# Chunk 1 of the first feed-forward layer in seven block products, with weight sums ahead, x inside `big`, and a new planned order

## Chip, core and metric

The kernel runs on one core of a Trainium2 chip: TensorE (PE, with its weight loads shown as PEld), VectorE (DVE), ScalarE (ACT), GpSimd (POOL) and SyncE (SP, which only issues DMAs here). The metric is the device time of one execution in microseconds (us). The kernel before took 268.82 us, the median of three runs between 268.78 and 269.34.

## What is computed

Four layers on x, 2048 tokens of 512 in bf16: linear attention, feed-forward, and both again with the same weights (wqkv 512 x 1536, wo 512 x 512, w1 512 x 1376, w2 1376 x 512).

```python
def _A_ref(x, wqkv, wo):          # 32 heads of 16
    qkv = (x @ wqkv).reshape(B, S, 3, H, Dh).transpose(2, 0, 3, 1, 4)
    q, k, v = qkv[0], qkv[1], qkv[2]
    phi = lambda t: jnp.where(t > 0, t + 1, jnp.exp(t)) + 1e-6
    pq, pk = phi(q), phi(k)
    kv = jnp.einsum("bhsd,bhse->bhde", pk, v)
    z = jnp.einsum("bhsd->bhd", pk)
    num = jnp.einsum("bhqd,bhde->bhqe", pq, kv)
    den = jnp.einsum("bhqd,bhd->bhq", pq, z)[..., None] + 1e-6
    return (num / den).transpose(0, 2, 1, 3).reshape(B, S, D) @ wo

def _B_ref(x, w1, w2):
    h = jnp.maximum(jnp.einsum("bsd,df->bsf", x, w1), 0)
    return jnp.einsum("bsf,fd->bsd", h, w2)

x = x + _A_ref(_layernorm(x), wqkv, wo)
x = x + _B_ref(_layernorm(x), w1, w2)
x = x + _A_ref(_layernorm(x), wqkv, wo)
x = x + _B_ref(_layernorm(x), w1, w2)
```

## The kernel before

**Tiles and tensors.** The tokens lie in 16 tiles of 128 tokens, four tiles to a chunk. `xin` holds x as loaded, `xres` the running sum in f32, `xn` the normalised tokens in f16, `Tb` the same transposed. `big` holds 48 units of 128 x 512 in bf16: pk and pq in attention (units 0 to 31), the spread reciprocals in units 32 to 47, and in a feed-forward layer h, where unit `c * 4 + t` is block c of 128 features for chunk t (c runs from 0 to 10, the last one with 96 features). `escr` and `lnd` are scratch.

**Attention** (layers 0 and 2): `a_k` and `a_q` project with wqkv and `phi_evac` evacuates from PSUM: ACT writes x + 1 (`_lin`) and exp (`_exp`), DVE takes the minimum (`_em`) and the maximum (`_phi`). `a_g` sums pk against the tokens over all chunks, `bar` closes these sums and forms `Mf` from them (`a_g_evac`, `a_kv`, `a_m` with its mask on DVE at L728, evacuation at L735 and L736). `a_den` forms the denominators, `a_spread` spreads their reciprocals by DMA (L783), `a_pqs` multiplies pq by them (L789), and `a_fin_chunk` multiplies by `Mf` and adds to the stream (`resid`, L660), with squares on ACT (L668) and the statistics and norms of the next layer (`ln_half`, `ln_stats` L572 to L584, `ln_norm` L590 to L599, transposes by DMA at L604).

**Feed-forward** (layers 1 and 3): a chunk's h = relu(x w1) is made either by `b_h`, block by block (four matmuls of 512 columns for each of ten blocks, relu at L964 or L965), or by `b_h7`, which cuts tokens, inputs and features in two each and needs seven block products instead of eight (a Strassen-Winograd scheme). For this it forms four sums of the tokens (`hs1` to `hs4`, L888) and four sums of w1 (`usum1` to `usum4`, L866), saves three products from PSUM by ACT (L926), adds in PSUM and by DVE (L913) and applies the relus (L916, L917, L943, L945). Each product has 10 matmuls of 256 columns. The 96 features left over go through `b_h_rest` and a DMA transpose (L844). The second half, h times w2, is always in seven products (`b_out`), with sums of h (`ssum1` to `ssum5`, `ssumr`) and of w2 (`wsum1` to `wsum6`; these two kinds at L983, the sign change `wsum6` at L995), and evacuations at L1066, L1074, L1082 and L1085. `H7_FROM = 2`: in layer 1 chunks 0 and 1 go through `b_h`, chunks 2 and 3 through `b_h7`; layer 3 uses `b_h7` throughout. The sums of w1 and w2 are written over `xin` once it is dead, apart from `usum3` and `wsum3`, which overwrite a quarter of w1 and of w2.

**Order.** The program records operations with what they read and write (`_Graph`), each with an assumed duration, and `_list_schedule` then puts them in an order for each engine: at each step, of the first so many operations not yet issued on an engine (`WINDOW`), by priority, the one that can start first. The priority is the place in the program plus an entry of the table `HINTS`; an entry with "!" fixes the engine of an operation that may run on several (`add_flex`: the number counts the alternatives). Operations with names in `LOCKED` are kept from running on DVE and POOL at the same time in that plan. Each engine then runs its list strictly in order, waiting on semaphores. `layer_steps` gives steps with what they need, so that the layers interleave.

Of the kernel before, what the change touches and what calls it, by code (L numbers as in the profile page):

```python
# [7 lines left out]
ALU = alu_op_type.AluOpType  # L8
# [38 lines left out]
TAIL = {PE: 150.0, ACT: 125.0, DVE: 80.0, POOL: 40.0, SP: 0.0}  # L47
# [4 lines left out]
WINDOW = {PE: 64, ACT: 80, DVE: 80, POOL: 12, SP: 6}  # L52


HINTS = {"0.bnag10": 2, "0.bnag14": 17, "0.bnst10": -271, "0.bnst12": 80, "0.bnst14": 51, "0.bnst15": 33, "0.bnst6": -82,
# [294 lines left out]
def build_kernel(nc, A_x, A_wqkv, A_wo, B_w1, B_w2, out, n_layers_pairs=2, K_STT=0, Q_STT=0, windows=None,  # L350
# [14 lines left out]
    EPS = 1e-5  # L365
    INV_D = 1.0 / D
    NLAYERS = 2 * n_layers_pairs
    UNITS = max(8 + 4, NFC) * NCH

    es = contextlib.ExitStack()  # L370
    with es:
# [14 lines left out]
        NL = 2  # L386
        FIN_SPLIT = 4
        SPLIT_H = 4
        H7_FROM = 2
        MID_FIRST = ()  # L390
        MID_LAST = ()
        FIRST_ACT_TILES = 4
# [1011 lines left out]
```

## Time and profile before

| | |
|---|---|
| median of the runs | 268.82 us (268.78 to 269.34) |
| the profiled execution | 269.65 us, of which the span of instructions is 267.9 us |
| matmuls and weight loads | 2020 each |
| DVE, ACT, POOL instructions | 612, 420, 158 |
| DMA | 22.18 MB, 83 GB/s mean |
| DMA issues on SP | three of wqkv and six of x in the first 6 us, 32 spreads, 28 transposes of `xn`, 8 of `hr` |

All times in the text count from the first instruction of the span. "busy" sums may overlap: a matmul's record is longer than the distance to the next one, because matmuls are pipelined. An idle engine costs nothing by itself; what counts is whether the engine that sets the end waits.

### The profile page before, as it was taken

To read this page: it belongs to the slowest core of one execution; us is meant where nothing else is said; L and a number is where in the kernel's file an instruction comes from. 1 tells how busy PE (TensorE), PEld (TensorE's weight loads), DVE (VectorE), ACT (ScalarE), POOL (GpSimd) and SP (SyncE) were. 2 spreads that over 40 slices of the span, in tenths; PEclk is the share of its full clock that TensorE was granted. 3 is DMA by queue.
4 is the path that set the end of the run, shared out by engine and by line. 5 is a ranking of instruction groups with operands and counts; after the bars stand their busy time and mean duration, and the time that the engine had idled before them with its cause. 6 is when DMAs were issued, how large, how long until landed. Compare 5 with 4: busy or idle time off the path is not lost.

```text
span 267.9 us, 5482 instructions
## 1 busy us (share of the span) xinstructions
PE 262.3 (98%) x2020; PEld 183.8 (69%) x2020; DVE 220.5 (82%) x612; ACT 192.0 (72%) x420; POOL 62.8 (23%) x158
## 2 busy tenths in 40 slices
PE   7999999999999999999999999999999999999995
PEld 3665446744646798768687745764488788898884
DVE  5799695679998799698889676348998989899994
ACT  4999987475994467689947599687899886475600
POOL 3210000015678014204005440000760830000000
PEclk9999999999999999999999999999999999999999
DMA  6904490644992400502202222063273221511012
GB/s 201 356 9 92 71 305 0 157 110 88 246 129 51 91 20 4 98 4 39 39 2 39 42 40 39 0 142 96 57 144 79 40 42 42 134 22 78 2 78 81
DMA packets 44890, 22.18 MB, mean 83 GB/s; under 512 B 34784, under 2 KB 43328, under 8 KB 44864
## 3 DMA queue, kind: packets, MB, share of 16 engines
q1 hardware_dynamic: 44864, 21.83, 34.5%
q8 instruction: 16, 0.26, 0.4%
q14 instruction: 10, 0.08, 0.1%
HBM read 7.14 MB, written 2.10 MB: 34 GB/s over the span
## 4 chain that ended last, share of the span: by engine, by line
PE 79%; ACT 8%; DMA 6%; DVE 5%; issue 0%; SPq 0%; DVEq 0%
PE ps L653 79%; DMA Tb<-xn 3%; ACT big L636 2%; ACT sqscr L668 2%; DMA wvl<-in_A_wqkv_dram 2%; DVE xres L660 2%; DMA xin<-in_A_x_dram 1%; ACT escr L638 1%; DVE big L789 1%; ACT Tb L624 1%; ACT xn L599 1%; DVE xn L590 1%; DVE bst L552 1%; ACT xres L638 1%; DVE xn L594 0%
## 5 line engine op out<-in xcount | busy, mean ns | idle before, releaser
L636 ACT ACTIVATE big<-ps 128x512 bf16<-128x512 f32 x64 | 39.7, 644 | 6.1 <-PE ps L653 5.8
L653 PE MATMUL ps<-Tb,w 128*128 128x256 f16 (+1 forms) x216 | 35.8, 304 | 0.1
L668 ACT ACTIVATE sqscr<-xres 128x512 bf16<-128x512 f32 x48 | 30.0, 626 | 6.9 <-DVE xres L1085 4.2
L653 PE MATMUL ps<-w,big 128*128 128x256 bf16 (+1 forms) x256 | 32.4, 272 | 0.0
L653 PE MATMUL ps<-wqkv,Tb 128*128 128x512 bf16 x128 | 31.2, 379 | 0.6 <-DMA Tb<-xn 0.6
L653 PE MATMUL ps<-big,xn 128*128 128x256 bf16 (+1 forms) x224 | 31.6, 288 | 0.0
L653 PE MATMUL ps<-Tb,wqkv 128*128 128x512 f16 (+1 forms) x144 | 31.4, 355 | 0.0
L638 ACT ACTIVATE escr<-ps 128x512 bf16<-128x512 f32 x48 | 29.9, 637 | 1.1 <-PE ps L653 1.1
L653 PE MATMUL ps<-Mf,big 128*128 128x512 bf16 x128 | 29.5, 379 | 0.0
L926 ACT ACTIVATE escr<-ps 128x512 f32<-128x512 f32 (+1 forms) x40 | 20.3, 540 | 11.2 <-PE ps L653 10.9
L653 PEld LDWEIGHTS ps<-w,big 128*128 128x128 bf16 (+1 forms) x256 | 25.0, 98 | 3.7
L653 PEld LDWEIGHTS ps<-big,xn 128*128 128x128 f16 x224 | 21.4, 98 | 8.8 <-issue 0.7
L653 PEld LDWEIGHTS ps<-Tb,w 128*128 128x128 bf16 x216 | 20.8, 98 | 9.5 <-DMA Tb<-xn 1.0
L913 DVE TENSOR_TENSOR big<-ps,escr 128x512 bf16<-128x512 f32 (+1 forms) x40 | 24.0, 606 | 3.7 <-PE ps L653 1.8
L599 ACT ACTIVATE xn<-xres,nbias,rstd 128x512 f16<-128x512 f32 x19 | 15.2, 810 | 9.6 <-POOL nbias L584 6.7
L653 PEld LDWEIGHTS ps<-Tb,wqkv 128*128 128x128 bf16 x144 | 13.9, 98 | 11.9 <-issue 0.2
L653 PEld LDWEIGHTS ps<-Mf,big 128*128 128x128 bf16 x128 | 12.2, 98 | 14.0 <-issue 0.7
L916 ACT ACTIVATE big<-big 128x512 bf16<-128x512 bf16 (+1 forms) x34 | 19.0, 569 | 3.2 <-DVE big L913 2.9
L646 DVE TENSOR_TENSOR big<-big,escr 128x512 bf16<-128x512 bf16 x48 | 19.8, 420 | 1.6 <-ACT big L636 1.1
L653 PEld LDWEIGHTS ps<-wqkv,Tb 128*128 128x128 f16 x128 | 12.1, 98 | 12.8 <-ACT escr L638 1.1
L1066 DVE TENSOR_TENSOR xres<-ps,xres 128x512 f32<-128x512 f32 x24 | 16.4, 685 | 4.6 <-PE ps L653 4.5
L640 DVE TENSOR_SCALAR escr<-escr 128x512 bf16<-128x512 bf16 x48 | 13.7, 287 | 7.7 <-ACT escr L638 7.2
(116 smaller groups left out, 525.2 us busy)
## 6 DMA issues: line engine op xcount, KB each, us to landing
big<-rdc SPq DMA_DIRECT2D x32, 128.0 KB, 2.6
wqkv<-in_A_wqkv_dram SPq DMA_DIRECT2D x3, 512.0 KB, 6.8
xin<-in_A_x_dram SPq DMA_DIRECT2D x3, 512.0 KB, 7.6
w<-in_B_w_dram SPq DMA_DIRECT2D x1, 1376.0 KB, 6.3
w<-in_B_w_dram SPq DMA_DIRECT2D x1, 1280.0 KB, 7.1
wo<-in_A_wo_dram SPq DMA_DIRECT2D x1, 512.0 KB, 7.2
out_dram<-GT SPq DMA_DIRECT2D x1, 512.0 KB, 2.6
out_dram<-Mf SPq DMA_DIRECT2D x1, 512.0 KB, 2.6
```

What stands on the lines that cost most here:

```text
L599: (ACT, lambda e: e.activation(xn[:, i, :], src, ACTF.Identity, scale=rstd[:, i:i + 1], bias=nbias[:, i:i + 1]), C_ACT_SB_AP)],
L636: g.add(ACT, lambda e: e.activation(dst_ap, psv[:, b, :], ACTF.Identity, bias=1.0 + 1e-6, scale=1.0), [("ps", b)], [dst_key], C_ACT_PSUM, ...
L638: g.add(ACT, lambda e: e.activation(sap, psv[:, b, :], ACTF.Exp), [("ps", b)], skeys, C_ACT_EXP, name=name + "_exp")
L640: g.add(DVE, lambda e: e.tensor_scalar(sap, sap, 1.0, 1e-6, ALU.min, ALU.add), skeys, skeys, C_DVE_BF4X, name=name + "_em")
L646: g.add(DVE, lambda e: e.tensor_tensor(dst_ap, dst_ap, sap, ALU.max), [dst_key] + skeys, [dst_key], 340.0, name=name + "_phi")
L653: last = e.matmul(o, l, r, start=st, stop=sp, skip_group_check=skip)
L660: g.add(DVE, lambda e: e.scalar_tensor_tensor(xres[:, i, :], psv[:, b, :], 0.0, src, ALU.add, ALU.add, accum_out=s1[:, i:i + 1]), [("ps", ...
L668: g.add(ACT, lambda e: e.activation(sqscr[:, q, :], xres[:, i, :], ACTF.Square, scale=math.sqrt(INV_D), accum_out=s2[:, i:i + 1]), xr(i), ...
L913: g.add(DVE, lambda e: e.tensor_tensor(ap, sh(psv[:, bank, 0:w]), sh(other()), ALU.add), [("ps", bank)] + okeys + ([] if first else bk), q ...
L916: g.add_flex([(ACT, lambda e: e.activation(ap, ap, ACTF.Relu), C_ACT_PSUM if len(cs) == 2 else 270.0), (DVE, lambda e: e.tensor_scalar(ap, ...
L926: g.add(ACT, lambda e, w=w: e.activation(q[:, 0:w], psv[:, bank, 0:w], ACTF.Identity), [("ps", bank)], key, C_ACT_PSUM if len(cs) == 2 els ...
L1066: g.add(DVE, lambda e: e.tensor_tensor(dst, psv[:, bank, :].rearrange("p (a k) -> p a k", k=256), dst, ALU.add), [("ps", bank)] + keys, ke ...
```

## The change

1. `H7_FROM` goes from 2 to 1: in layer 1 chunk 1 too goes through `b_h7`.
2. The sums of w1 have a tensor of their own, `tws`, those of w2 another, `tw2s`. All of them but `usum3` move from layer 1 into `bar` of layer 0; `usum3` stays ahead of chunk 1's `b_h7`.
3. `xin` is no tensor of its own any more but units 32 to 47 of `big`. h's blocks 8 to 10 lie there (`h_key` makes their writers wait for the readers of x), and the spread reciprocals move from there to the tiles of `Tb` of the same chunk (`rb_ap`).
4. `pqs`, `hs`, `ssum`, `usum` and `wsum` may run on DVE or POOL, a norm on DVE, ACT or POOL (before: every fourth on POOL, the others on DVE or ACT). `pool_tt` is the planner's assumed duration for POOL.
5. The planner's constants change (end of a matmul 150 to 160, a norm on DVE 530 to 470, POOL's window 12 to 40), and so does the place of layer 1's steps: its first is recorded after layer 0's third chunk instead of the second, and its first output step has no condition any more.
6. `HINTS` is replaced (494 entries before, 443 after).

```diff
-TAIL = {PE: 150.0, ACT: 125.0, DVE: 80.0, POOL: 40.0, SP: 0.0}
+TAIL = {PE: 160.0, ACT: 125.0, DVE: 80.0, POOL: 40.0, SP: 0.0}
-WINDOW = {PE: 64, ACT: 80, DVE: 80, POOL: 12, SP: 6}
+def pool_tt(cols):
+    return 2.2 * cols + 90.0
+WINDOW = {PE: 64, ACT: 80, DVE: 80, POOL: 40, SP: 6}
...
-    UNITS = max(8 + 4, NFC) * NCH
+    UNITS = 8 * NCH + NT
-        xin = sb("xin", [128, NT, 512], BF16)
-        H7_FROM = 2
+        H7_FROM = 1
+        xin = big[:, 8 * NCH * 512:UNITS * 512].rearrange("p (n d) -> p n d", d=512)
+        tws = sb("tws", [128, 3 * 1280], BF16)
+        tw2s = sb("tw2s", [128, 4096], BF16)
+        def h_key(u):
+            return [("big", u)] + ([("xin", u - 8 * NCH)] if u >= 8 * NCH else [])
...
-            if i % 4 == 3:
-                g.add(POOL, ts[1], xr(i) + [("rstd", i), ("mean", i)], [("xn", i)], ts[2], name="norm%d" % i)
-                return
-            g.add_flex([(DVE, ts[1], 530.0),
-                        (ACT, lambda e: e.activation(...), C_ACT_SB_AP)],
+            g.add_flex([(DVE, ts[1], 470.0),
+                        (ACT, lambda e: e.activation(...), C_ACT_SB_AP), ts],
...
-        def rb_unit(t, j):
-            return 32 + 4 * j + t
+        def rb_ap(t, j):
+            return Tb[:, 4 * t + j, :, :].rearrange("p c k -> p (c k)").bitcast(BF16)
-                    [("rdc", t)], [("big", u)], 650.0, "spread%d_%d" % (t, j), issue=620.0, late=late)
+                    [("rdc", t)], [("T", 4 * t + j)], 650.0, "spread%d_%d" % (t, j), issue=620.0, late=late)
+                f = (lambda e, u=u, j=j: e.tensor_tensor(unit_ap(u), unit_ap(u), rb_ap(t, j), ALU.mult))
+                g.add_flex([(DVE, f, 340.0), (POOL, f, pool_tt(512))], [("T", 4 * t + j), ("big", u)], [("big", u)], name="pqs%d_%d" % (t, j))
...
-        def w1_sums():
+        def w1_sums(part):
...
+                if (nm == "usum3") == (part == 0) and part < 2:
+                    continue
+                f = (lambda e, o=o, a=a, b=b: e.tensor_tensor(o, a, b, ALU.subtract))
+                g.add_flex([(DVE, f, C_DVE_SUM), (POOL, f, pool_tt(1280))], rd, wr, name=nm)
...
-                g.add(DVE, lambda e, o=o, a=a, b=b, op=op: e.tensor_tensor(o, a, b, op), rd, [wr], 340.0, name="%s_%d" % (nm, t))
+                f = (lambda e, o=o, a=a, b=b, op=op: e.tensor_tensor(o, a, b, op))
+                g.add_flex([(DVE, f, 340.0), (POOL, f, pool_tt(512))], rd, [wr], name="%s_%d" % (nm, t))
...
         def tt(out_, a, b, op, reads, writes, dur, name):
-            g.add(DVE, lambda e: e.tensor_tensor(out_, a, b, op), reads, writes, dur, name=name)
+            cols = {C_DVE_SUM: 1280, 450.0: 768, 340.0: 512, 200.0: 256}[dur]
+            f = (lambda e: e.tensor_tensor(out_, a, b, op))
+            g.add_flex([(DVE, f, dur), (POOL, f, pool_tt(cols))], reads, writes, name=name)
...
                 def bar():
                     g_a(NCH - 1)
+                    if first_layer:
+                        tw7.append(w1_sums(2 if H7_FROM == 0 else 0))
+                        w2_sums()
...
-                    if first_b and t == 0:
-                        w2_sums()
                     b_out(t, last_layer, sums[t])
...
                     if last_layer or t >= H7_FROM:
-                        if not tw7:
-                            tw7.append(w1_sums())
+                        if first_b and t == H7_FROM and t > 0:
+                            w1_sums(1)
                         b_h7(t, tw7[0])
...
-                    steps.append((1 if first_b and t == 0 else t, None, lambda t=t: h_step(t)))
+                    steps.append((2 if first_b and t == 0 else t, None, lambda t=t: h_step(t)))
                     if t >= 1:
-                        steps.append((NCH - 1 if first_b and t == 1 else None, None if last_layer else t - 1, lambda t=t: o_step(t - 1)))
+                        steps.append((None, None if last_layer else t - 1, lambda t=t: o_step(t - 1)))
```

The entries of the table that fix a sum on POOL are `hs1_3`, `hs3_2`, `hs4_1`, `ssum3_3`, `ssum4_0`, `ssumr_3` in layer 1 and `hs1_2`, `hs2_3`, `hs3_2`, `hs4_2`, `ssum4_0`, `ssum4_1`, `ssum5_2`, `ssumr_0` in layer 3 (the last number is the chunk). Of the loads, w1 loses its entry (231 before), w2's goes from 424 to 198, wo's from 239 to 156, wvl's from 164 to 190, and x's last quarter gets 146.

More of the change, by code (lines that the diff above doesn't have):

```diff
@@ L51 @@
 C_POOL_ADD = 1250.0
-WINDOW = {PE: 64, ACT: 80, DVE: 80, POOL: 12, SP: 6}
-HINTS = {"0.bnag10": 2, "0.bnag14": 17, "0.bnst10": -271, "0.bnst12": 80, "0.bnst14": 51, "0.bnst15": 33, "0.bnst6": -82,
[74 rows of a table removed]
+def pool_tt(cols):
+    return 2.2 * cols + 90.0
+WINDOW = {PE: 64, ACT: 80, DVE: 80, POOL: 40, SP: 6}
+HINTS = {"0.bnag11": 144, "0.bnst10": 103, "0.bnst8": 75, "0.bnst9": 111, "0.den1": 95, "0.fin0_2": -280, "0.fin14_0": 193,
[66 rows of a table added]
 class _Op:
@@ L367, in build_kernel @@
     NLAYERS = 2 * n_layers_pairs
-    UNITS = max(8 + 4, NFC) * NCH
+    UNITS = 8 * NCH + NT
+    assert NFC * NCH <= UNITS
     es = contextlib.ExitStack()
@@ L594, in ln_norm @@
             ts = (POOL, lambda e: e.tensor_scalar(xn[:, i, :], src, mean[:, i:i + 1], rstd[:, i:i + 1], ALU.add, ALU.mult), C_POOL_NORM)
-            if i % 4 == 3:
-                g.add(POOL, ts[1], xr(i) + [("rstd", i), ("mean", i)], [("xn", i)], ts[2], name="norm%d" % i)
-                return
-            g.add_flex([(DVE, ts[1], 530.0),
-                        (ACT, lambda e: e.activation(xn[:, i, :], src, ACTF.Identity, scale=rstd[:, i:i + 1], bias=nbias[:, i:i + 1]), C_ACT_SB_AP)],
+            g.add_flex([(DVE, ts[1], 470.0),
+                        (ACT, lambda e: e.activation(xn[:, i, :], src, ACTF.Identity, scale=rstd[:, i:i + 1], bias=nbias[:, i:i + 1]), C_ACT_SB_AP), ts],
                        xr(i) + [("rstd", i), ("mean", i), ("nbias", i - i % 2)], [("xn", i)], name="norm%d" % i)
@@ L781, in a_spread @@
             for j in range(4):
-                u = rb_unit(t, j)
-                dma(lambda e, j=j, u=u: e.dma_start(unit_ap(u), rdc[32 * j:32 * j + 32, t, :].unsqueeze(1).broadcast_to([32, 4, 512])),
-                    [("rdc", t)], [("big", u)], 650.0, "spread%d_%d" % (t, j), issue=620.0, late=late)
+                dma(lambda e, j=j: e.dma_start(rb_ap(t, j), rdc[32 * j:32 * j + 32, t, :].unsqueeze(1).broadcast_to([32, 4, 512])),
+                    [("rdc", t)], [("T", 4 * t + j)], 650.0, "spread%d_%d" % (t, j), issue=620.0, late=late)
         def a_pqs(t):
             for j in range(4):
-                u, r = pq_unit(j, t), rb_unit(t, j)
-                g.add(DVE, lambda e, u=u, r=r: e.tensor_tensor(unit_ap(u), unit_ap(u), unit_ap(r), ALU.mult),
-                      [("big", r), ("big", u)], [("big", u)], 340.0, name="pqs%d_%d" % (t, j))
+                u = pq_unit(j, t)
+                f = (lambda e, u=u, j=j: e.tensor_tensor(unit_ap(u), unit_ap(u), rb_ap(t, j), ALU.mult))
+                g.add_flex([(DVE, f, 340.0), (POOL, f, pool_tt(512))], [("T", 4 * t + j), ("big", u)], [("big", u)], name="pqs%d_%d" % (t, j))
         def a_fin_mm(i, b, js):
@@ L845, in b_h_rest @@
                                                 hr[:, s, :, :].rearrange("p i f -> p (i f)")),
-                [("hr", s)], [("big", u)], 450.0, "trh%d" % t)
+                [("hr", s)], h_key(u), 450.0, "trh%d" % t)
         KH = (NFC - 1) // 2
         wqf = wqkv[:].rearrange("p c n -> p (c n)")
-        xinf = xin[:].rearrange("p n d -> p (n d)")
         HT = 2 * KH * 128
-        def w1_sums():
+        def w1_sums(part):
             def blk(k):
-                return xinf[:, HT * k:HT * (k + 1)].rearrange("p (d f) -> p d f", d=2)
+                return tws[:, HT * k:HT * (k + 1)].rearrange("p (d f) -> p d f", d=2)
             n = KH * 128
@@ L858, in w1_sums @@
             b12, b22 = w1[:, 0:2, n:2 * n], w1[:, 2:4, n:2 * n]
-            def wk(lo, hi):
-                return [("xin", i) for i in range(lo, hi)]
             t1, t2, t4 = blk(0), blk(1), blk(2)
-            for (o, a, b, rd, wr, nm) in ((t1, b12, b11, [("w1",)], [("uw", 1)] + wk(0, 3), "usum1"),
-                                          (t2, b22, t1, [("w1",), ("uw", 1)], [("uw", 2)] + wk(3, 5), "usum2"),
+            for (o, a, b, rd, wr, nm) in ((t1, b12, b11, [("w1",)], [("uw", 1)], "usum1"),
+                                          (t2, b22, t1, [("w1",), ("uw", 1)], [("uw", 2)], "usum2"),
                                           (b12, b22, b12, [("uw", 1)], [("uw", 3), ("w1",)], "usum3"),
-                                          (t4, b21, t2, [("w1",), ("uw", 2)], [("uw", 4)] + wk(5, 8), "usum4")):
-                g.add(DVE, lambda e, o=o, a=a, b=b: e.tensor_tensor(o, a, b, ALU.subtract), rd, wr, C_DVE_SUM, name=nm)
+                                          (t4, b21, t2, [("w1",), ("uw", 2)], [("uw", 4)], "usum4")):
+                if (nm == "usum3") == (part == 0) and part < 2:
+                    continue
+                f = (lambda e, o=o, a=a, b=b: e.tensor_tensor(o, a, b, ALU.subtract))
+                g.add_flex([(DVE, f, C_DVE_SUM), (POOL, f, pool_tt(1280))], rd, wr, name=nm)
             return t1, t2, b12, t4
@@ L904, in quarter @@
                 us = [h_unit(c0 + p, t) for p in range(len(cs))]
-                return ap, [("bq", u, half) for u in us], [("big", u) for u in us]
+                return ap, [("bq", u, half) for u in us], [k for u in us for k in h_key(u)]
             def add(name, cs, bank, other, okeys, second, half, first):
@@ L966, in b_h @@
                              C_DVE_FLEX)],
-                           [("ps", b)], [("big", u)], name="hrelu%d_%d" % (t, c))
+                           [("ps", b)], h_key(u), name="hrelu%d_%d" % (t, c))
         xnb = xn[:].bitcast(BF16)
         HN = KH * 256
-        assert NFC == 2 * KH + 1 and FLAST < 128 and 3 * HN + 256 <= 4096 and HN <= 2048
+        assert KH == 5 and NFC == 2 * KH + 1 and FLAST < 128 and 3 * HN + 256 <= 4096 and HN <= 2048
         def xblk(o, n=KH):
-            return xinf[:, o:o + n * 256].rearrange("p (c k) -> p c k", k=256)
-        tw1, tw2, tw4 = xblk(4096), xblk(4096 + HN), xblk(4096 + 2 * HN)
-        tw1r = xinf[0:FLAST, 4096 + 3 * HN:4096 + 3 * HN + 256]
+            return tw2s[:, o:o + n * 256].rearrange("p (c k) -> p c k", k=256)
+        tw1, tw2, tw4 = xblk(0), xblk(HN), xblk(2 * HN)
+        tw1r = tw2s[0:FLAST, 3 * HN:3 * HN + 256]
         st_rdc = (rdc, lambda il, hf: [("rdc", il)])
@@ L987, in w2_sums @@
             b12, b22 = w2[:, 0:KH, 256:512], w2[:, KH:2 * KH, 256:512]
-            xk = [("xin", i) for i in range(8, NT)]
-            tt(tw1, b12, b11, ALU.subtract, [("w2a",)], [("tw", 1)] + xk, C_DVE_SUM, "wsum1")
+            tt(tw1, b12, b11, ALU.subtract, [("w2a",)], [("tw", 1)], C_DVE_SUM, "wsum1")
             tt(tw2, b22, tw1, ALU.subtract, [("w2a",), ("tw", 1)], [("tw", 2)], C_DVE_SUM, "wsum2")
```

140 rows, old and new, of the table HINTS are left out of this document.

## The prediction, made before the changed kernel ran

> **What bounds the kernel now.** I read the engine totals first, then the chain that ended last, then TensorE's instructions in order of time.
>
> ```profile
> span 267.9 us, 5482 instructions
> PE 262.3 (98%) x2020; PEld 183.8 (69%) x2020; DVE 220.5 (82%) x612; ACT 192.0 (72%) x420; POOL 62.8 (23%) x158
> ```
>
> ```profile
> 24.66 4.66 DMA wvl<-in_A_wqkv_dram
> ...
> 30.12 3.19 DMA Tb<-xn
> 33.30 0.14 issue
> 33.44 23.72 PE ps L653 x168
> ...
> 73.72 4.11 DMA Tb<-xn
> 77.82 0.05 issue
> 77.87 187.03 PE ps L653 x1540
> 264.90 0.02 issue
> 264.93 0.42 DVE rdc L1082
> ```
>
> From 33.44 us on, the chain is TensorE except between 57 and 78 us, where it runs through DVE, ACT and a transposing DMA, and TensorE has its own work even there. Busy time of pipelined matmuls overlaps, so I take their price from start to start. In TensorE's own order:
>
> ```profile
> 56.11 11.40 PE L653 MATMUL ps<-Mf,big 128*128 128x512 bf16 x52
> 67.34 0.50 PE L653 MATMUL ps<-w,Tb 128*128 128x96 bf16 x8
> ...
> 177.33 2.78 PE L653 MATMUL ps<-big,xn 128*128 128x256 bf16 x24
> 179.95 0.39 PE L653 MATMUL ps<-GT,wqkv 128*128 128x128 bf16 x4
> ```
>
> (67.34 - 56.11) / 52 = 216 ns for one of 512 columns; (179.95 - 177.33) / 24 = 109 ns for one of 256. Going through the stream with these prices I find one hole of size in the bulk (0.75 us before 33.44, the wait for the transposes of chunk 3) and one of 0.3 us at 77.5. So TensorE's work sets the time from 33 us to 264.9, and a matmul taken out is worth what it takes, as long as DVE, ACT and POOL keep feeding it.
>
> **Chunk 1 in seven products.** It removes the 40 matmuls of 512 columns of `b_h(1)` and adds 7 products of 10 matmuls of 256 columns:
>
> 40 x 0.216 - 70 x 0.109 = 8.64 - 7.63 = 1.01 us less on TensorE.
>
> The 96 columns left over (`b_h_rest`) stay. This lies wholly on the path. What it adds elsewhere, by the rows of the six chunks that already do this (mean of one; 512 and 256 columns): nine saves by ACT, 6 x 0.60 + 3 x 0.40 = 4.8; nine adds from PSUM by DVE, 6 x 0.69 + 3 x 0.42 = 5.4; their nine relus, 5.1 on ACT or 2.4 on DVE; three direct relus, 1.6 on ACT; four sums `hs`, 4 x 0.42 = 1.7. Ten relus of about 0.6 go, 6.0. Net 10 to 13 us over three engines, and here is what has room:
>
> ```profile
> 33.40:50.00 16.60, 16.56 (x116) 10.30 (x117) 11.65 (x38) 11.72 (x24) 0.39 (x1) 1.00 0.53 157
> 50.00:57.00 7.00, 7.00 (x55) 3.80 (x54) 4.76 (x13) 4.90 (x10) 0.00 (x0) 1.00 0.37 83
> 57.00:67.00 10.00, 10.00 (x48) 4.58 (x47) 9.82 (x30) 5.62 (x14) 4.36 (x13) 1.00 0.56 126
> 67.00:78.00 11.00, 10.85 (x80) 6.67 (x79) 10.38 (x33) 10.73 (x28) 8.08 (x18) 1.00 1.03 205
> 78.00:88.00 10.00, 10.00 (x70) 5.95 (x69) 9.23 (x20) 5.93 (x13) 6.93 (x10) 1.00 0.41 78
> ```
>
> Columns: stretch, its length, then busy PE, PE weight loads, DVE, ACT, POOL, the clock (1.00 throughout), DMA. From 57 to 88 us DVE is idle for only 31 - 29.4 = 1.6 us, ACT for 8.7, POOL for 11.6. Alone, the new 7 us of DVE would not fit.
>
> **The weight sums moved ahead.** They make the room. In the trace DVE does seven of the nine sums of w1 and w2, and the sign change, between 72.4 and 87 us: 6 x 0.82 + 0.28 + 0.37 = 5.6 us. They go into `bar` of layer 0 (`usum3` alone stays, since it overwrites weights that chunk 0 still needs). That leaves DVE 1.6 + 5.6 = 7.2 us from 57 to 88, against 5.4 + 1.7 + 2.4 less some 2 us of relus that go, 7.5. It fits about evenly, with the rest spilling past 88, where the flexible relus can go to ACT and sums to POOL. I put this at nothing; the cover is that room, and if it is gone, each us by which DVE falls short stands on TensorE, because a group holds three of eight PSUM banks until its adds are done.
>
> Where the sums go, 7 x 0.82 + 0.28 + 0.37 = 6.4 us with `usum4`, DVE is idle for 16.6 - 11.65 + 7.0 - 4.76 = 7.2 us, and in `bar` it waits for TensorE anyway (1.38 and 0.73 us before 48.92 and 50.68). A sum that starts just ahead of one of the four DVE steps of that chain (L717, L728 twice, L736) delays it by up to 0.82: between 0 and 3.3 us if all four are hit and TensorE has nothing else. It has, projections and `den`; I take 0.
>
> **Loads.** The sums need w1 and w2 early. SP's order follows the planner's rule: lowest priority number first, within a window of six, unready operations included. By hand this gives the trace of before (wvl behind the first two transposes, w1 behind the next two), so I use it for the new numbers: w1 comes into the first burst, ahead of x's last quarter, and wo, wvl, w2 behind chunk 2's transposes, near 24.7 us.
>
> ```profile
> 24.66 0.58 SPq L497 DMA_DIRECT2D wvl<-in_A_wqkv_dram  x1
> ...
> 32.78 0.58 SPq L502 DMA_DIRECT2D w<-in_B_w_dram  x1
> ...
> 67.45 0.58 SPq L503 DMA_DIRECT2D w<-in_B_w_dram  x1
> ```
>
> w1 in front of x's last quarter: a quarter lands 7.6 us after an issue by 5.7 us, w1 adds up to its own 6.3, so 19.6 at the latest; the last four `bn_stats` start between 19.7 and 24.8. Nothing, though it is near. w2 (7.1 us to land) then crosses the transposes of chunk 3, queued on the same SP queue, which TensorE already waits for at 33.44. Bounds: a gain of 0.75 if the new order ends that wait, a loss of 1.1 (below). I take 0.
>
> **x in the room of `big`, reciprocals in `Tb`.** h's units 32 to 43 now wait for the residuals that read x; the twelfth of these ends at 68.3 us, chunk 0's last relus run after 75. The spreads write `Tb` tiles whose projections ended long before 45.8, and the transposes that refill them wait for `pqs`, done by 54 us for chunks 0 and 1, by 61 and 64 for the others, where those transposes are issued from 63.19, 71.56 and 77.97 on. Nothing; if `pqs` comes late, the transposes behind it on SP are late with it.
>
> **Sums and norms on POOL.** This is the part without a row: POOL does no wide two-input operation now. Its widest, a norm with one input of 512 columns, takes 0.77 us undisturbed; a second input costs between nothing and as much again, so 1.5 to 3.0 ns a column. But the rows show that POOL and DVE hold each other up:
>
> ```profile
> 64.71 0.58 DVE L584 TENSOR_TENSOR nbias<-mean,rstd 128x2 f32<-128x2 f32 x1
> ...
> 78.94 0.81 DVE L983 TENSOR_TENSOR xin<-w,xin 128x1280 bf16<-128x1280 bf16 x1
> ```
>
> ```profile
> 64.52 0.77 POOL L594 TENSOR_SCALAR xn<-xres,mean,rstd 128x512 f16<-128x512 f32 x1
> ...
> 78.97 0.84 POOL L578 TENSOR_TENSOR var<-s,nm 128x2 f32<-128x2 f32 x1 [1.35 <-ACT sqscr L668]
> ```
>
> A two-column `nbias` on DVE, 0.15 elsewhere, takes 0.58 and ends with POOL's norm at 65.29; a two-column `var` on POOL, 0.20 elsewhere, takes 0.84 beside DVE's sum. A two-input operation on either side waits out the other; those that read PSUM (L965 at 71.45, 0.68 beside a norm) don't. So a sum given to POOL frees 0.42 us of DVE only where DVE has PSUM work to do meanwhile. Between a gain of nothing (TensorE has no holes to fill) and the loss worked out below, I take 0, since the order forbids such overlaps in its plan. The Trainium skill (SBUF — State Buffer, section "SBUF: two separate sides") calls this pair of ports an exclusive lock held for a whole instruction, and by that rule every sum on POOL stops DVE's two-input work; the trace agrees, 0.58 against 0.15, and the rule's result is the second rival.
>
> **Sum.** In the profiled execution's own terms, 269.65 (span 267.9) - 1.01 = 268.6; that execution was 0.83 over the median, 268.82, so a median of 267.8.
>
> **Rivals.** (1) The order also closes holes: 0.75 + 0.3 more, 266.8. For it: the wait at 33.44 hangs on wvl landing at 29.3, an accident of DMA. Against: w2 now travels there.
>
> (2) Slower: POOL's sums stop DVE in the last layer. The new table fixes on POOL four `hs`, two `ssum4`, one `ssum5`, one `ssumr` there, 4 x 512 + 2 x 768 + 512 + 256 = 4352 columns: at 2.25 ns, 9.8 us. DVE is rid of 4 x 0.42 + 2 x 0.55 + 0.42 + 0.28 = 3.5. If DVE stands through all of it, it loses 6.3; its idle time from 206 to 254 is 48 - (14.5 + 15.0 + 14.9) = 3.7 us. TensorE is late by the rest, 2.6: 270.4. It decides once the stops pass 3.7 us. Against: much of DVE's work there reads PSUM.
>
> (3) No change: wo, wvl and w2, 1.9 MB behind one another from 24.7 us, hold up chunk 3's transposes. w2 alone lands 7.1 us after its issue near 25.8; wo ahead of it adds 512 KB at the best slice's 356 GB/s, 1.4: 34.4 against a landing at 33.3 now, so TensorE waits 1.1 longer and the gain is spent: 268.9.
>
> **Chances.** The plain sum 50% (267.3 to 268.2 by itself), rival 1 12%, rival 2 24%, rival 3 14%. A measurement of this kernel can tell about 0.2%, 0.54 us, from no change: faster 62%, same 14%, slower 24%. The range runs from just under rival 1 to rival 2, 266.7 to 270.3; the four hits in `bar` at once and a total standstill of DVE are left out.
>
> **What would show it.** Matmuls of 512 columns on `Tb,w` fall from 64 to 24 and those of 256 grow by 70; PE's stream from 33 to 265 us shorter by 1.0 with no new hole. Wrong steps would show as PE waits: on DVE `big` or `hs` near 80 us, on DMA `Tb<-xn` near 33, or DVE sums far over 0.42 beside POOL sums after 206. A hole over 1 us anywhere after 33 makes the prediction wrong.

## The result, and the profile after

The changed kernel took **295.02 us** (294.60 to 297.00, 6 runs) beside 268.80 (268.30 to 271.29, 6 runs) for the kernel before on the same chip: ratio 1.0968, 95% interval 1.0918 to 1.1019. It is 26 us slower, where 267.8 was predicted and 266.7 to 270.3 given as the range. The profiled execution took 294.87 us, its span 293.1.

The totals of the changed kernel, with the clock that TensorE was granted in slices of 7.3 us:

```profile
span 293.1 us, 5616 instructions
...
PE 268.7 (92%) x2050; PEld 185.2 (63%) x2050; DVE 239.1 (82%) x635; ACT 199.6 (68%) x417; POOL 84.1 (29%) x174
...
PEclk9779799999999999999999999999999999999999
```

The clock falls to seven tenths in the second, third and fifth slice (nine or more throughout before), and TensorE is busy for 92% of the span where it was 98%. The clock itself is little of the loss: the two executions of the changed kernel that were granted 0.994 on average took 294.60 and 294.64 us, the profiled one with 0.981 took 294.87. TensorE's groups of matmuls in the first feed-forward's products on `Tb,w` (changed kernel, then kernel before: count, busy us and mean ns, idle time before them):

```profile
L654 PE MATMUL ps<-Tb,w 128*128 128x512 f16 x24 | 5.7, 379 | 0.0
```

```profile
L653 PE MATMUL ps<-Tb,w 128*128 128x512 f16 x64 | 15.1, 379 | 0.1
```

Forty matmuls of 512 columns are gone, as planned; over all operands, those of 512 columns fell from 480 to 440 and those of 256 grew by 70 (2050 matmuls in all). The loss lies elsewhere. The chain of waits, which before was TensorE's from 33.44 us on except between 57 and 78, now reads (start, length, what):

```profile
4.18 1.28 ACT L564
5.70 1.28 ACT L562
7.21 1.28 ACT L564
...
28.64 1.28 ACT L639
...
37.53 1.28 ACT L639
46.98 4.85 DMA Tb<-xn
51.87 11.02 PE ps L654 x74
...
166.36 3.18 DVE nbias L588
170.89 49.74 PE ps L654 x344
```

Two things are new in it: a row of pieces of 1.28 us on ACT with no tile to their name, and 3.18 us of a two-column `nbias`. The wait for chunk 3's transposes ends at 51.87 instead of 33.44 (at 51.87 it is their second half that TensorE waits for; the first half is used from 46.30 on). ACT's groups say what the pieces are (line, operation, count, then busy us and mean ns):

```profile
L562 ACT ACT_TABLE_LOAD x6 | 7.7, 1283 | 0.9 <-PEq L1392 0.8
...
L564 ACT ACT_TABLE_LOAD x4 | 5.1, 1283 | 0.1
...
L639 ACT ACT_TABLE_LOAD x2 | 2.6, 1283 | 0.0
...
L515 ACT ACT_TABLE_LOAD x1 | 1.3, 1283 | 0.0
```

Thirteen loads of ScalarE's function tables, where the kernel before has one, at 1.05 us. ACT in order of time:

```profile
3.96 0.20 ACT L562 ACTIVATE veps<-mv 128x1 f32<-128x1 f32 x1 [1.90 <-DVE mv L557]
4.18 1.28 ACT L564 ACT_TABLE_LOAD   x1
5.48 0.20 ACT L564 ACTIVATE rstd<-veps 128x1 f32<-128x1 f32 x1
5.70 1.28 ACT L562 ACT_TABLE_LOAD   x1
6.99 0.20 ACT L562 ACTIVATE veps<-mv 128x1 f32<-128x1 f32 x1
7.21 1.28 ACT L564 ACT_TABLE_LOAD   x1
```

Here each `veps` (Ln, L562) and each `rstd` (Exp, L564) has a load of its own in front: the two functions of 0.20 us are 1.28 us apart. (Later, at 28.64 and 37.53, it is an attention exponential at L639 that brings the load back to Exp.) What waits for it is DVE, then TensorE:

```profile
L594 DVE TENSOR_SCALAR xn<-big,mv,rstd 128x512 f16<-128x512 bf16 x16 | 6.1, 408 | 14.2 <-ACT rstd L564 14.1
```

```profile
9.22 0.61 PE L619 MATMUL ps<-ident,xn 128*128 128x128 f16 x4 [2.41 <-DVE xn L594]
...
16.24 0.61 PE L619 MATMUL ps<-ident,xn 128*128 128x128 f16 x4 [2.25 <-DVE xn L594]
```

The sixteen first norms on DVE stand 14.1 us for `rstd`, and TensorE for the norms; by stretches (length, busy PE, weight loads, DVE, ACT, POOL, clock, DMA) the first 33.4 us are, after and before:

```profile
0.00:33.40 33.40, 23.14 (x129) 12.00 (x130) 17.50 (x53) 29.69 (x51) 4.55 (x17) 0.89 0.47 160
```

```profile
0.00:33.40 33.40, 30.96 (x188) 17.06 (x188) 26.26 (x86) 29.34 (x67) 5.53 (x19) 1.00 0.54 146
```

TensorE does 129 matmuls instead of 188 there, and ACT is just as full, of loads.

**Where they come from.** `_table` (L515) loads one set that holds both Ln and Exp. The new `HINTS` has an entry that the old one lacks, `"0.table": 577`. It moves this operation from first on ACT to the 76th place, at 56.98 us, behind 28 of the 32 attention exponentials of layer 0. In front of it, no common set is chosen, and a load stands at every change between Ln and Exp. The planner could not see this: it has 1.7 us for the operation wherever it stands, and nothing for a change of function.

### The profile page after: what moved, and what is told of

It reads as the page before. It is cut to its first block, busy times and chain, and to the rows that moved or that the text cites. A ratio compares the mean times of both kernels' runs of the same rounds, so it can differ in the third digit from the quotient of the medians.

```text
span 293.1 us, 5616 instructions
## 1 busy us (share of the span) xinstructions
PE 268.7 (92%) x2050; PEld 185.2 (63%) x2050; DVE 239.1 (82%) x635; ACT 199.6 (68%) x417; POOL 84.1 (29%) x174
## 4 chain that ended last, share of the span: by engine, by line
PE 59%; ACT 17%; DVE 13%; DMA 6%; POOL 2%; SPq 1%; issue 1%; DVEq 0%; POOLq 0%
PE ps L654 58%; DMA Tb<-xn 4%; ACT big L637 3%; ACT L562 2%; DVE Tb L985 2%; ACT L564 2%; DVE big L914 2%; ACT sqscr L669 2%; ACT xres L639 2%; DMA Tb<-rdc 1%; ACT escr L639 1%; DVE xres L661 1%; DVE nbias L588 1%; SPq L783 1%; DVE big L918 1%
## 5 line engine op out<-in xcount | busy, mean ns | idle before, releaser
L654 PE MATMUL ps<-wqkv,Tb 128*128 128x512 bf16 x128 | 32.9, 398 | 2.4 <-DMA Tb<-xn 1.5
L654 PE MATMUL ps<-big,xn 128*128 128x256 bf16 (+1 forms) x224 | 33.0, 298 | 2.2 <-DVE big L647 2.2
L654 PE MATMUL ps<-Tb,w 128*128 128x256 f16 (+1 forms) x196 | 30.0, 286 | 1.1 <-DVE w L865 0.6
L914 DVE TENSOR_TENSOR big<-ps,escr 128x512 bf16<-128x512 f32 (+1 forms) x47 | 27.7, 598 | 3.7 <-ACT escr L927 2.3
L639 ACT ACTIVATE escr<-ps 128x512 bf16<-128x512 f32 x48 | 29.7, 639 | 0.5 <-PE ps L654 0.2
L654 PEld LDWEIGHTS ps<-w,big 128*128 128x128 bf16 (+1 forms) x256 | 24.8, 98 | 3.7 <-ACT big L965 0.3
L927 ACT ACTIVATE escr<-ps 128x512 f32<-128x512 f32 (+1 forms) x47 | 23.8, 540 | 2.2 <-PE ps L654 1.6
L917 ACT ACTIVATE big<-big 128x512 bf16<-128x512 bf16 (+1 forms) x29 | 16.5, 575 | 9.9 <-DVE big L914 9.8
L654 PEld LDWEIGHTS ps<-Tb,w 128*128 128x128 bf16 x196 | 18.4, 98 | 7.5 <-DVE w L865 0.9
L654 PE MATMUL ps<-xn,w 128*128 128x256 f16 x140 | 20.1, 273 | 1.1 <-ACT lnd L927 1.1
L586 POOL TENSOR_TENSOR rstd<-veps,nhalf 128x2 f32<-128x2 f32 x24 | 17.9, 750 | 11.1 <-DVE veps L584 10.4
L654 PE MATMUL ps<-xn,tws 128*128 128x256 f16 x140 | 19.8, 273 | 0.5 <-ACT big L944 0.5
```

Source lines behind the costliest of these rows:

```text
L586: g.add(POOL, lambda e: e.tensor_tensor(rstd[:, sl], veps[:, sl], nhalf[:, 0:n], ALU.pow), [("veps", lo), ("nhalf",)], [("rstd", i) for i ...
L639: g.add(ACT, lambda e: e.activation(sap, psv[:, b, :], ACTF.Exp), [("ps", b)], skeys, C_ACT_EXP, name=name + "_exp")
L654: last = e.matmul(o, l, r, start=st, stop=sp, skip_group_check=skip)
L914: g.add(DVE, lambda e: e.tensor_tensor(ap, sh(psv[:, bank, 0:w]), sh(other()), ALU.add), [("ps", bank)] + okeys + ([] if first else bk), q ...
L917: g.add_flex([(ACT, lambda e: e.activation(ap, ap, ACTF.Relu), C_ACT_PSUM if len(cs) == 2 else 270.0), (DVE, lambda e: e.tensor_scalar(ap, ...
L927: g.add(ACT, lambda e, w=w: e.activation(q[:, 0:w], psv[:, bank, 0:w], ACTF.Identity), [("ps", bank)], key, C_ACT_PSUM if len(cs) == 2 els ...
```

## Experiments

All runs stand beside the kernel before, on the same chip, 268.93 to 269.06 us in the medians of each group.

**The table load alone, both ways.** The first kernel leaves all lists as they are and only loads the common set at the head of ACT; the second is the kernel *before* with its load moved to where the new table of hints puts it.

```diff
+            if e == ACT:
+                handle.add_instruction(mybir.InstLoadActFuncSet(act_func_set_id=LN_EXP_SET, ...))
             for o in order[e]:
...
         def _table(e):
-            e.add_instruction(mybir.InstLoadActFuncSet(...))
             return e.activation(lnw[:], nhalf[:, 0:2], ACTF.Square)
```

> The changed kernel, its order untouched, but the load of the table set that holds both Ln and Exp stands first on ACT instead of 76th. Theory T (tables): until the explicit load at 57 us, each switch between Ln and Exp loads a table, 12 loads more than before, 12 x 1.283 = 15.4 us, and they lie on the chain; the wait for chunk 3 comes 18.4 us later than before (51.87 against 33.44). So 295.0 falls by 15 to 18.5: 276.5 to 280. Rival L (loads): w1 and w2 brought ahead hold up the first stage; then it stays above 290. Rival P (POOL): the loss is spread over the run through sums on POOL; then it stays above 285.

```diff
+        late = next(o for o in order[ACT] if o.name == "table")
+        order[ACT].remove(late)
+        place = next(k for k, o in enumerate(order[ACT]) if o.key == "0.q3_1_exp")
+        order[ACT].insert(place + 1, late)
```

> The kernel before, its order untouched, but the table load and its small activation moved behind the exp of q3_1, where the changed kernel has them. Theory T: 268.8 + 15 to 18.5 = 284 to 287.5. Rivals L and P: nothing else is changed, so no more than one load of 1.3 us in mid-stream, up to 270.1.

Measured: 282.34 us (281.54 to 283.79; ratio 1.0496, 1.0452 to 1.0540) for the first, 12.7 less than the changed kernel, and 285.28 (284.22 to 286.15; 1.0598, 1.0557 to 1.0638) for the second, 16.4 more than the kernel before. One load and thirteen:

```profile
L1333 ACT ACT_TABLE_LOAD x1 | 1.3, 1283 | 0.8 <-PEq L1395 0.8
```

```profile
L558 ACT ACT_TABLE_LOAD x6 | 7.7, 1283 | 0.9 <-PEq L1394 0.8
L560 ACT ACT_TABLE_LOAD x5 | 6.4, 1283 | 0.1
...
L638 ACT ACT_TABLE_LOAD x1 | 1.3, 1283 | 0.0
L511 ACT ACT_TABLE_LOAD x1 | 1.3, 1283 | 0.0
```

The place of one instruction costs the old kernel 16 us, so it needs nothing of the change's other parts. The first kernel came out over its expectation: 12 loads more are 12 x 1.283 = 15.4 us of ACT, of which 12.7 reach the end. The last wait for chunk 3's transposes ends at 39.22 there, not at 33.44: something else keeps it 5.8 us.

**The entry alone.** The changed kernel without `"0.table"`, its order planned anew:

```diff
-HINTS = {... "0.table": 577, ...}
+HINTS = {... ...}
```

> The changed kernel without the one entry 0.table (577) of the table of orders, planned anew, so that the load stands first and the rest of the order shifts with it. Theory T: within 2 us of the first run, 275 to 281. If the rest of the order is fitted to this entry, it is slower than the first by more.

283.79 us (282.35 to 285.68): one load, at the start. It is over the expected band, as the first kernel is, and 1.5 us above that kernel, with ranges that overlap. So the entry is all of this cause, and 13 to 15 us are left beyond the kernel before.

**The sums on POOL.** Around the other long piece of the chain, changed kernel, POOL and DVE:

```profile
166.30 0.66 POOL L985 TENSOR_TENSOR Tb<-big 96x256 bf16<-96x256 bf16 x1
166.36 3.18 DVE L588 TENSOR_TENSOR nbias<-mean,rstd 128x2 f32<-128x2 f32 x1 [0.60 <-POOL rstd L586]
...
166.93 2.59 POOL L985 TENSOR_TENSOR big<-big 128x1280 bf16<-128x1280 bf16 x1
...
170.89 0.28 PE L654 MATMUL ps<-tw2s,xn 128*128 128x256 bf16 x1 [2.32 <-DVE xres L1068]
```

`nbias` on DVE, 0.15 us elsewhere, starts 0.06 after the first of two sums on POOL and ends at 169.54 with the second (166.93 + 2.59 = 169.52); ACT's norm waits for it, and so does the rest of DVE's list, with the `xres` of L1068 for which TensorE stands 2.32 us. Counted over all DVE instructions that exceed the shortest of the same line and shape by more than 0.05 us, five lines give 12.3 us of this: L985 4.1, `nbias` 3.0, the relus of L918 2.7, `var` 1.5, `hs` 1.0. Next, one kernel moves all these sums (`pqs`, `hs`, `ssum`, `usum`, `wsum`) to DVE, by their planned start, on top of the early table load; another only `ssum3` of layer 1's chunk 3.

```diff
+        for o in [o for o in order[POOL] if o.name.startswith(("pqs", "hs", "ssum", "usum", "wsum"))]:
+            order[POOL].remove(o)
+            o.eng = DVE
+            order[DVE].append(o)
+        order[DVE].sort(key=lambda o: (o.t_start, o.idx))
```

> As the first, and every sum and pqs that the plan gave to POOL is put into DVE's list at the place of its planned start; all other lists stay. It tells apart what is left over the kernel before (some 9 us). Theory P: POOL's 28 us of wide two-input operations hold DVE up; with them gone from POOL it is 3 to 8 us faster than the first. Rival D (DVE is full): DVE takes some 9.6 us more work and falls behind; 1 to 6 us slower than the first. Within 1 us of the first: the left-over lies in the order itself.

> The kernel with the table load first (282.34 us) and one sum moved: ssum3 of layer 1's chunk 3 (POOL at 154.32, 2.59 us, L985, with its 0.66 us piece ahead) goes to VectorE. Theory P (a wide sum on POOL holds a VectorE instruction that runs beside it): nbias at L588, 3.17 us beside it, goes back to about 0.15, TensorE's hole of 2.32 us ahead of the matmuls at 158.3 shrinks to under 0.7, and VectorE's own 1.0 us for the sum eats a part: 280.0 to 281.2 us. Rival D (VectorE is what is short here, and POOL took load off it): the statistics come as late as before, the hole keeps 1.5 us or more, and the time is 281.8 to 283.3.

276.21 us (275.52 to 276.53; 1.0259, 1.0225 to 1.0292), 6.1 less, although DVE has 657 instructions where it had 635 (the five lines' 12.3 us are 0.2 there); and 279.99 (279.83 to 280.55), 2.4 less, for the one sum. The same place with that sum on DVE:

```profile
153.06 0.66 POOL L985 TENSOR_TENSOR Tb<-big 96x256 bf16<-96x256 bf16 x1
153.12 0.62 DVE L588 TENSOR_TENSOR nbias<-mean,rstd 128x2 f32<-128x2 f32 x1 [0.60 <-POOL rstd L586]
...
154.34 0.81 DVE L985 TENSOR_TENSOR big<-big 128x1280 bf16<-128x1280 bf16 x1
...
155.81 0.72 PE L654 MATMUL ps<-tw2s,xn 128*128 128x256 bf16 x5 [0.49 <-DVE xres L1068]
```

`nbias` waits out the one piece left on POOL, 0.62, the sum takes 0.81 instead of 2.59, and TensorE's hole falls from 2.32 to 0.49. Is this loss a part of the first? The changed kernel with its late table load, and only the sums moved:

> The changed kernel (295.02 us) with its late table load, and only the sums moved from POOL to VectorE. Theory A (the two causes stand apart: the table loads cost before 57 us, POOL's sums after it): 6 us less, as between the first two kernels with the table load in front: 288 to 290.5 us. Rival M (the table loads have made other engines wait and so hide a part of what POOL's sums cost): less than 3 us, 292 to 295.

288.42 us (288.11 to 288.59), 6.6 less: the two causes add up. Compared matmul by matmul with the changed kernel, the gain comes in three places: 2.5 us near 100, 2.3 near 169 and 1.3 near 230 us, the last layer. Near 100, in the changed kernel, a sum of 256 columns took DVE 1.72 us beside one of 2.15 on POOL, and TensorE stood 1.64 us for it.

**The load of wvl.** In the kernel with both cures, SP's issues, and DVE behind them:

```profile
22.29 0.58 SPq L503 DMA_DIRECT2D wo<-in_A_wo_dram  x1
22.91 0.53 SPq L501 DMA_DIRECT2D wvl<-in_A_wqkv_dram  x1
23.48 0.43 SPq L507 DMA_DIRECT2D w<-in_B_w_dram  x1
25.92 10.36 SPq L605 DMA_TRANSPOSE Tb<-xn  x2
```

```profile
29.11 0.76 DVE L680 TENSOR_TENSOR wqkv<-wqkv,wvl 128x512 bf16<-128x512 bf16 x2 [2.89 <-DMA wvl<-in_A_wqkv_dram]
...
33.89 0.81 DVE L985 TENSOR_TENSOR tw2s<-w 128x1280 bf16<-128x1280 bf16 x1
34.62 0.40 DVE L594 TENSOR_SCALAR xn<-big,mv,rstd 128x512 f16<-128x512 bf16 x1
```

```profile
33.80 1.90 PE L654 MATMUL ps<-wqkv,Tb 128*128 128x512 bf16 x8 [1.80 <-DMA Tb<-xn]
...
39.11 1.90 PE L654 MATMUL ps<-wqkv,Tb 128*128 128x512 bf16 x8 [1.24 <-DMA Tb<-xn]
```

DVE waits for wvl until 29.11, as before (2.20 us, until 29.34). But before, chunk 3's last norm followed 1.4 us later, at 30.73. Here 5.5 us of other work on DVE stand between, a weight sum among them, so the norm runs at 34.62, 3.9 us later, and the transposes behind it, which TensorE waits for, are used from 39.11 on. The other half of chunk 3's transposes was issued long before, behind the load of w2 (at 25.92), and TensorE waits for it too, 1.80 us until 33.80; but what sets the time is the half that comes last.

```diff
+        wl = next(o for o in order[SP] if o.name == "ld_wvl")
+        order[SP].remove(wl)
+        place = next(k for k, o in enumerate(order[SP]) if o.name == "ld_wv0")
+        order[SP].insert(place + 1, wl)
```

> The kernel with the table load first and the sums on VectorE (276.21 us), with one more edit: the load of wvl (L501) is issued right behind wv's, in the first burst, and no longer behind wo. Theory W (the late wvl holds VectorE): the wait of 2.89 us at L680 falls below 0.5, chunk 3's last norm and transposes come 2 to 3 us earlier (they landed at 39.1), and TensorE's two holes of 1.97 at 31.6 and 1.4 at 37.6 shrink by as much together: 273.2 to 274.4 us. Rival Q (the transposes of chunk 3 are held by the load of w2 ahead of them in SyncE's list and on the DMA engines): the wait at L680 goes, the transposes still land near 39, and the time stays between 275.6 and 276.6. Rival E (one load more in the first burst delays the first tiles): TensorE starts its matmuls on chunk 2 later by 0.5 to 1 us and the time is 276.5 to 277.2.

273.91 us (273.12 to 274.20; 1.0163, 1.0129 to 1.0197), 2.3 less. The norm runs at 31.63 and the last half of chunk 3 starts at 36.99; the other half starts at 31.64, without a hole.

**What the order is worth.** 5 us are left, and TensorE's stream shows where, from start to start: holes of 11.9 us in all, against 6.8 before, the large ones at 35.4 (1.45 us, transposes), from 80 to 86 (1.5 us, chunk 1's sums on DVE), at 204 (0.57) and at 220 (1.04). (A hole is what the distance between two starts exceeds the usual one by.) Less the holes, its stream is 269.0 - 11.9 = 257.1 us, before 264.9 - 6.8 = 258.1: the 1.0 us of chunk 1 is there. So I kept the instructions and rearranged the five lists by a local search (single instructions are moved within their list, or to another engine that may run them, the sums excepted; a move stays mostly where the planned end comes earlier). DVE's and ACT's planned durations are raised by 3 to 5 per cent, since 234 us of DVE were measured where 227 were planned. The edit replaces each list:

```diff
+        for e, lst in ORDER.items():
+            order[e] = [g.ops[i] for i in lst]
+            for o in order[e]:
+                if o.eng != e:
+                    o.eng, o.emit, o.dur = next(x for x in o.alts if x[0] == e)
```

The run e7 does this to the kernel with wvl early, e8 to the same with `H7_FROM = 2`, e9 to the kernel before:

> The kernel with the table load first, the sums on VectorE and wvl's load early (273.91 us), with the same instructions on the same data but each engine's list rearranged by a local search, in which no sum goes to POOL and VectorE's and ScalarE's planned durations are raised by 3 to 5 per cent. Theory S (chunk 1 in seven products is worth the 1.0 us that TensorE saves, and all that was lost lay in the table loads, in POOL's sums and in the order): TensorE's holes fall from 11.9 us to between 5 and 6.5 (before: 6.8), and the time is 266.0 to 267.6 us, below the kernel before. Rival D (VectorE, 234 us busy of 272, is now too full, and some of the holes at 80 to 92, 204 and 220 stay in any order): 268.9 to 271 us.

> As the run e7, but H7_FROM is 2: chunk 1 of layer 1 goes through the plain products again, all else of the change stays, and each engine's list is rearranged by the same search. Theory S: 40 matmuls of 512 columns more and 70 of 256 less, 0.9 to 1.3 us above e7. Rival D (the 14 sums, copies and adds that chunk 1 no longer needs take load off VectorE and ScalarE): not above e7, and up to 1 us below it.

> The kernel before, with each engine's list rearranged by the same search and nothing else: what of e7's gain is the search's and not the change's. Theory S: of before's 6.8 us of holes 4.0 lie in the first 33 us, where the loads set the pace, so that at most 1.5 us can be won: 267.4 to 269.0 us, 0.7 us or more above e7. Rival O (the order alone is what matters): within 0.4 us of e7.

268.46 us (267.44 to 269.40, 12 runs; ratio 0.9981, 0.9962 to 1.0001), 271.15 (270.45 to 271.94; 1.0080, 1.0053 to 1.0106) and 268.82 (268.31 to 270.92, 12 runs; 1.0008, 0.9986 to 1.0030). The order alone brings 5.4 us. The first misses its expected band, though rival D's too. It lies only 0.36 us below the third, with ranges that overlap: that is rival O's outcome (within 0.4), not the 0.7 that theory S asked for. The second, 2.7 above the first, can't be read as a price of chunk 1: its search started from a worse order, planned with the places of layer 0 and the choices of engine alone out of the hints, and left holes of 1.3 us at 24.8 and 0.9 at 157.9. A second search, with a changed goal, for the pair that can be compared, e11 (the change) and e12 (before):

> The same instructions as the run e7 (268.46 us), rearranged anew: the search now also keeps POOL's norms from running beside VectorE's work on SBUF, and lets the transposes land up to 0.4 us later. Theory S: a little better than e7, 267.4 to 268.3 us, and 0.3 us or more below e12. Rival D (VectorE is too full for any order to do better): 268.3 to 269.2.

> The kernel before, rearranged by this second search: the pair of e11. Theory S: 268.0 to 269.0 us, 0.3 us or more above e11. Rival O (the change's 1.0 us on TensorE is eaten by the work that it adds on VectorE and ScalarE, so that only the order counts): within 0.3 us of e11, or below it.

**268.10 us** (267.72 to 268.46, 12 runs; ratio 0.9960, 0.9942 to 0.9978) and 268.86 (268.33 to 269.71, 12 runs; 0.9993, 0.9972 to 1.0013). They lie 0.76 us apart, as theory S has it this time. The first is the only version whose interval lies below the kernel before, by 0.4%. Its totals and TensorE's waits:

```profile
span 266.0 us, 5606 instructions
...
PE 260.9 (98%) x2050; PEld 186.6 (70%) x2050; DVE 227.9 (86%) x646; ACT 188.7 (71%) x413; POOL 57.5 (22%) x155
```

```profile
PE ps L624 <- DVE wrm L617: 1.2, 1, 1.2
PE ps L753 <- DMA wqkv<-in_A_wqkv_dram: 0.4, 1, 0.4
PE ps L753 <- DVE xres L1167: 0.2, 1, 0.2
PE ps L718 <- DVE xn L693: 0.2, 1, 0.2
```

From 78 to 105 us, where the kernel with wvl early left holes, DVE is no less busy and TensorE never idle (second order, then the kernel with wvl early; columns as above):

```profile
78.00:105.00 27.00, 27.00 (x268) 24.05 (x267) 25.05 (x75) 18.93 (x40) 6.83 (x16) 1.00 0.23 45
```

```profile
78.00:105.00 27.00, 25.98 (x242) 21.08 (x241) 24.36 (x63) 14.37 (x30) 3.17 (x8) 1.00 0.20 42
```

From 295.02 to 268.10, then: table load 12.7, POOL's sums 6.1, wvl 2.3, order 5.8. (The steps were timed on several chips; on these the kernel before took 268.80 to 269.06.)

## Why the prediction was wrong

**The step that failed** is the sum, "269.65 (span 267.9) - 1.01 = 268.6". It has no term for the new table of hints, though the table was read for loads and for sums on POOL. An entry that the old table lacks, on an operation that looks like a warm-up, went unread, and so did what runs ahead of it then: Ln and Exp in turns. Twelve loads of 1.283 us, and 12.7 us at the end. The Trainium skill (ScalarE: Activation LUTs, section "Table sets: the hidden batching unit") says that Ln followed by Exp needs one load, since one set holds both; in these traces that is so only once that set was loaded explicitly (1 load against 13), and the measurement decides. The sum has no term for the rest of the new order either, and rearranging it brought 5.4 to 5.8 us.

**"Since the order forbids such overlaps in its plan"**, the ground for taking the sums on POOL at 0, failed second, at 6.1 us with a table load in front and 6.6 without. The plan keeps apart only operations whose names are in `LOCKED`; `nbias`, `var` and the relus on DVE aren't, and they made 7.3 of the 12.3 us. Those that are listed collide all the same (L985, 4.1 us): the plan's times aren't the chip's. There were also more sums on POOL than were counted, 22 in the trace where the table fixes 14; the planner put the other eight there by its own choice. The price was right: 1.28 us for 512 columns, 1.85 for 768, 2.59 for 1280, 2.0 to 2.5 ns a column within the 1.5 to 3.0 given. Rival 2 had the mechanism but put it in the last layer, at 2.6 us; it showed there with about 1.3, and in layer 1 with 2.5 and 2.3. The last of these was run by itself (2.4 us): it came through one held instruction that others waited for, not through DVE's total. And "two-input" was too narrow: the relus of L918 read one operand, and one of them took 1.15 us, 0.28 in the median, while POOL ran a sum of 1.14. The Trainium skill (SBUF — State Buffer, "SBUF: two separate sides") has the loser blocked for a whole instruction; the trace agrees, and shows it for two in a row, 3.18 us for work of 0.15.

**Loads, taken at 0** (bounds -0.75 and +1.1): outside the bounds, +2.3 by the run with wvl early. Rival 3's mechanism, transfers that hold up the transposes, fits the half that TensorE waited 1.80 us for, but the time was set by the other half, 5.3 us later: DVE waited for wvl as it had before, and the new list put more work between that and chunk 3's norm.

**Chunk 1, 1.01 us less on TensorE:** right on TensorE's stream, 257.1 against 258.1 us. At the end it stays open: the two kernels lie 0.36 us apart under the first search and 0.76 under the second (268.10 and 268.86), and the two orders of the changed kernel differ by 0.36 themselves, so a part of either gap can be the search. **"It fits about evenly"** for DVE from 57 to 88 us was right about the room, not about the planned order: even with the sums on DVE and wvl early it has 2.1 us of holes from 78 to 105, the second order 0.2. **The weight sums in `bar`** delayed none of its four steps by much (with the early table load, the only large holes from 33 to 57 us are those ahead of chunk 3's transposes); one of them cost 0.8 us ahead of a norm. x in `big` and the reciprocals in `Tb` show in no wait of TensorE's.

The prediction's own sign of error, a hole over 1 us after 33, came true ahead of 51.87 (1.51 us), 99.97 (1.11), 103.31 (1.64) and 170.89 (2.32). What stays open: which of the moves in the last 5.8 us count.

## What to carry to other kernels

When a change replaces a table of orders, read it entry by entry for operations that set a state of an engine, and ask what runs ahead of them now. A planner's exclusion holds only for what it lists and only as exactly as its durations; before a wide sum goes to GpSimd, look for the short VectorE instructions on SBUF beside it and who waits for them. And compare the two versions after the same effort on order, else the order is measured.

## What was unexpected in the hardware

Before the common set was loaded, each change from Ln to Exp or back took a load of 1.283 us, and the next one started 1.51 us later (5.70 to 7.21 us, with one function of 0.20 between), so that hardly anything beside the load and the function shows. TensorE's granted clock was 0.89 on average in the first 33.4 us and 0.94 from there to 57, where it stood idle between short pieces of work; in the profiled execution of the kernel with the early load, the same matmuls fed more steadily, it was 1.00 over the whole span. That the idle time causes the lower clock is argued from this alone, and it can't be all: the old kernel with the late load was granted 0.988 in two executions and 1.00 in two others.
